# Depthwise taps of the first quarter ahead of the FFT rows, and full-height products in the inverse transform

## The chip, the core and the metric

The kernel runs on one core of a Trainium2 chip. Its engines are TensorE (PE, matrix products into PSUM), VectorE (DVE), ScalarE (ACT), GpSimd (POOL) and the queues that issue transfers (SP above all). Each works through its own list of instructions in order and waits on semaphores for the others. The metric is device time in microseconds (us) for one execution; less is better.

## What is computed

The reference is an H3 block with a long convolution, followed by a dense layer, both with a LayerNorm ahead and a residual:

```
k_shift = sum over t<4 of k delayed by t, times shift_k[:, t]       # depthwise taps
kv      = k_shift * v
y       = irfft(rfft(pad(kv)) * rfft(pad(ssm_k)))[:S] + kv * ssm_D  # FFT length 4096
h       = x + layernorm(x) * y
out     = h + relu(layernorm(h) @ w1) @ w2
```

The sequence has 2048 tokens of 512 channels, the dense layer is 1376 wide, inputs and output are bf16.

## The kernel before

The Fourier transforms are done as matrix products in two stages, 64 x 64. The cosine and sine tables are made on the chip: DVE computes angles as integers (`cs_turns`, `cc_turns`, `_turns`: an addition and a bit-wise AND each), and ACT takes sines of them (`table`, called through `cc_part` for the later pieces). POOL makes negated copies of the sine table (`negated`).

There is no automatic schedule: every engine runs its instructions in the order in which the program names them, so the order of the source is the order on each engine.

The stretch at the start, up to about 40 us:

- SP's queue issues the load of ssm_k (`sk`, 2 MB, L96), then transposing loads of k and v in quarters of 512 tokens, k0, v0, k1, v1 and so on (L113 to L118), then ssm_D (`draw`, L121). The tap weights (`wsh`, 4 KB) go through ACT's queue (L98).
- PE runs 22 warm-up matmuls on zeros (L110).
- POOL builds an identity, then for each of four channel groups the four diagonal matrices of tap weights (`wdiag`, L238), by which PE applies the taps.
- When ssm_k is there, `to_rows` (L277) turns it over: PE transposes words of two bf16 values (`pst`, L281) in eight groups, and DVE or ACT copies each group to the rows tile `kfl` (L284, L290; the letters D and A in L342 say who). PSUM holds three double banks (`ps0` to `ps2`, handed out in a ring by `place`) and two single ones (`pk0`, `pk1`).
- Then come eight rounds (L377). Round gb does the taps of two channel groups of quarter gb // 2 (`taps`: eight matmuls into `pk0` and `pk1`, and two DVE products with v from PSUM into `kvp2`, the place of kv in ssm_k's tile), and `stage1` of the FFT of ssm_k for eight columns: 64 small matmuls into two double banks, each copied to the table `a1` by ACT or DVE (`copy`, L259, L261). In rounds 0 to 5 ACT also takes one of six sines (`cc_part`).
- Then kv is turned to rows in the same way (L403 and L404), and stage 2 of ssm_k's transform follows, mixed with stage 1 of kv's (L410 to L421). Its DVE part adds ssm_D (`dtab`, which POOL prepares at L399) to the real part.

The product of the spectra and the inverse of stage 2 follow (L439 to L501). The inverse of stage 1 (`inv1`, L599) uses the tables `dre` and `dim`, of which the lower 64 rows hold a block for one half of the columns, the upper 64 rows for the other half, and the rest is zero. It multiplies the two halves of the rows separately: for each m and each of the two tables, two products with 64 rows and 128 columns, at two positions of PE's array. Sixteen steps b of four m each end in a copy to `ax`. `inv2_first` (L667) and the dense layer (`mlp1`, `mlp2`) follow and fill the rest, from about 110 us on.

Of the kernel before, what the change touches and what calls it, by code (L numbers as in the profile page):

```python
# [9 lines left out]
ALU = mybir.AluOpType  # L10
# [3 lines left out]
I32 = mybir.dt.int32  # L14
# [42 lines left out]
def kernel(  # L57
# [35 lines left out]


    sk = early.tile([P, DC, S], BF16, name="sk")
    nc.sync.dma_start(out=sk[:], in_=A_ssm_k.rearrange("(c p) t -> p c t", p=P))  # L96
    wsh = consts.tile([P, DC, KS], BF16, name="wsh")
    nc.scalar.dma_start(out=wsh[:], in_=A_shift_k.rearrange("(r p) j -> p r j", p=P))  # L98
    dtab = consts.tile([P, 64, DC], BF16, name="dtab")
    draw = consts.tile([P, DC, 64], BF16, name="draw")  # L100
    vT = [vp.tile([P, DC, 512], BF16, name=f"vT{c}") for c in range(4)]
# [1 line left out]
    kT = [(kvp if c < 2 else early).tile([P, DC, CH + 16], BF16, name=f"kT{c}") for c in range(4)]  # L103
    wdiag = kvp.tile([P, DC, KS, P], BF16, name="wdiag")

    idle = vT[3][:, 0, :]
    nc.vector.memset(idle, 0.0)
    warm = psum_t.tile([P, 512], F32, tag="pk0", name="warm")
    for _ in range(22):
        nc.tensor.matmul(out=warm[:], lhsT=idle[:, 0:P], rhs=idle, start=True, stop=True)  # L110

    nc.vector.memset(kT[0][:, :, 0:16], 0.0)
    for c in range(4):  # L113
        if c == 0:
            nc.sync.dma_start_transpose(out=kT[c][:, :, 16:CH + 16], in_=k_d[0:CH, :])  # L115
        else:
            nc.sync.dma_start_transpose(out=kT[c][:], in_=k_d[CH * c - 16:CH * c + CH, :])  # L117
        nc.sync.dma_start_transpose(out=vT[c][:], in_=v_d[CH * c:CH * c + CH, :])  # L118
    for dp in range(2):
        src = bass.AP(tensor=A_ssm_D.tensor, offset=A_ssm_D.offset + 64 * dp, ap=[[0, 64], [P, DC], [1, 64]])  # L120
        nc.sync.dma_start(out=draw[64 * dp:64 * dp + 64, :, :], in_=src)  # L121
# [28 lines left out]
    for s in range(0, P, 64):  # L150
# [5 lines left out]
    nc.gpsimd.memset(ident[:], 0.0)  # L156
    nc.gpsimd.affine_select(out=ident[:], in_=ident[:], compare_op=ALU.not_equal, fill=1.0,
                            base=0, pattern=[[-1, P]], channel_multiplier=1)
    ident32 = early.tile([P, P], F32, name="ident32")
    nc.gpsimd.tensor_copy(out=ident32[:], in_=ident[:])  # L160

    n1c = early.tile([P, 1], F32, name="n1c")
    n2c = early.tile([P, 1], F32, name="n2c")
# [14 lines left out]
    def at_k1(tab, k1):  # L178
        a, t = [p for p in tab if p[0] <= k1][-1]
        return t[:, k1 - a, :]  # L180

    tsn = early.tile([P, 32, 64], I32, name="w_ts")
    tcs = early.tile([P, 32, 64], I32, name="w_tc")
    ta = early.tile([P, 96], F32, name="w_ta")
# [18 lines left out]
    for dp in range(2):  # L203
        table(cs[0], tsn, dp)

    t1 = early.tile([P, 64], I32, name="f1_t")
    _turns(nc, t1[:, 0:32], r1[:], n1c[:], 128, True)
    _turns(nc, t1[:, 32:64], r1[:], n1c[:], 128, False)
    f1f = early.tile([P, 64], F32, name="f1_f")
    f1p = f1f[:].rearrange("p (k s) -> p s k", s=2)  # L210
    _sin(f1p[:, 0], t1[:, 0:32], 128)
    _sin(f1p[:, 1], t1[:, 32:64], 128, neg=True)
    t3 = early.tile([P, 2, 64], I32, name="dm_t")
    _turns(nc, t3[:, 0, :], r2[:, 32:96], n2s[:], 64, True)
    _turns(nc, t3[:, 1, :], r2[:, 32:96], n2s[:], 64, False)
    dsc = early.tile([P, 2, 64], F32, name="dm_f")
    cs_turns(*cs[1])
    cc_parts = [(cs[1], tsn, dp) for dp in range(2)] + [(p, tcs, dp) for p in cc for dp in range(2)]

    def cc_turns(a):  # L220
        part = tcs[:, a:a + 16, :]
        nc.vector.tensor_single_scalar(out=part, in_=tsn[:, a:a + 16, :], scalar=2048.0, op=ALU.add)
# [11 lines left out]
    for f in (f2hi, f2lo):  # L234
        nc.gpsimd.memset(f[:], 0.0)

    for rg in range(DC):
        nc.gpsimd.tensor_tensor(out=wdiag[:, rg, :, :], in0=ident[:].unsqueeze(1).to_broadcast([P, KS, P]),  # L238
                                in1=wsh[:, rg, :].unsqueeze(2).to_broadcast([P, KS, P]), op=ALU.mult)
        if rg == 1:  # L240
            nc.gpsimd.tensor_copy(out=f1hi[:, 0:64], in_=f1f[:])
            nc.gpsimd.tensor_tensor(out=f1f[:], in0=f1f[:], in1=f1hi[:, 0:64], op=ALU.subtract)
            nc.gpsimd.tensor_copy(out=f1lo[:, 0:64], in_=f1f[:])
# [27 lines left out]
    def bank2(name):  # L271
        return place([P, 2, 512], F32, name)
# [4 lines left out]
    def to_rows(word, q, fl, eng):  # L277
        shape = [P, 4, P]
        pst = tap_bank(q % 5 - 3, shape, F32, "pst") if word is sk_word and q % 5 > 2 else place(shape, F32, "pst")
        for i in range(4):  # L280
            nc.tensor.transpose(out=pst[:, i, :], in_=word(4 * q + i), identity=ident32[:])  # L281
        if eng == "D":
            fl32 = fl[:].rearrange("p g d n -> p (g d n)").bitcast(I32).rearrange("p (g d m) -> p g d m", g=64, d=2)
            nc.vector.tensor_single_scalar(out=fl32[:, :, :, 4 * q:4 * q + 4],  # L284
                                           in_=pst[:].bitcast(I32).rearrange("p m (d g) -> p g d m", d=2),
                                           scalar=0, op=ALU.bitwise_or)
        else:
            src = pst[:].rearrange("p m x -> p (m x)").bitcast(BF16).rearrange("p (m d g e) -> p d g m e", m=4, d=2, e=2)
            for d in range(2):
                nc.scalar.copy(out=fl[:, :, d, 8 * q:8 * q + 8].rearrange("p g (m e) -> p g m e", e=2), in_=src[:, d])  # L290
# [40 lines left out]
                             skip_group_check=True)  # L331


    kfl = early.tile([P, 64, 2, 64], BF16, name="kfl")
    sk32 = sk[:].rearrange("p c t -> p (c t)").bitcast(F32).rearrange("p (x m) -> p x m", m=32)
    kv32 = sk[:].rearrange("p c t -> p (c t)").bitcast(F32).rearrange("p (m x) -> p m x", m=32)

# [24 lines left out]


    kvp2 = sk[:].rearrange("p c t -> p (c t)").rearrange("p (m c a e) -> p m c a e", m=32, c=DC, e=2)
    def taps(c, h):
        pss = [tap_bank(i, [P, 512], F32, "pkv") for i in range(2)]
        for i in range(2):
            for j in range(KS):
                nc.tensor.matmul(out=pss[i][:], lhsT=wdiag[:, 2 * h + i, j, :],  # L369
                                 rhs=kT[c][:, 2 * h + i, 16 - j:CH + 16 - j], start=(j == 0), stop=(j == KS - 1))  # L370
        for i in range(2):
            nc.vector.tensor_tensor(out=kvp2[:, :, 2 * h + i, 8 * c:8 * c + 8, :].rearrange("p m a e -> p a m e"),  # L372
                                    in0=pss[i][:].rearrange("p (a m e) -> p a m e", a=8, e=2),
                                    in1=vT[c][:, 2 * h + i, :].rearrange("p (a m e) -> p a m e", a=8, e=2),
                                    op=ALU.mult)
# [222 lines left out]

    def inv1(b):  # L599
        if b < 15:  # L600
            ps = bank2("psi1")
            banks = (ps[:, 0], ps[:, 1])
        else:
            banks = (psum1.tile([P, 512], F32, tag="pm0", name="psi1a")[:], bank2("psi1b")[:, 0, :])
        for i in range(4):
            m = 4 * b + i
            for c, tab in ((0, dre), (1, dim)):
                for dp in range(2):
                    nc.tensor.matmul(out=banks[dp][:, 128 * i:128 * i + 128],  # L609
                                     lhsT=kf[halves[dp], c, 4 * m:4 * m + 4, :].rearrange("p r k -> p (r k)"),  # L610
                                     rhs=tab[halves[dp], dp].rearrange("p a b -> p (a b)"), start=(c == 0), stop=(c == 1),
                                     tile_position=(64 * dp, 0), skip_group_check=True)
# [231 lines left out]
```

## Time and profile before

| what | value |
|---|---|
| median of 3 runs | 203.83 us (203.73 to 203.92) |
| time of the profiled execution | 203.83 us |
| its span | 201.7 us |
| PE busy | 192.0 us (95%) |
| DVE busy | 145.3 us (72%) |
| ACT busy | 128.5 us (64%) |
| POOL busy | 86.5 us (43%) |

The span is the time between the first and the last instruction that the profile shows. A line of a timeline gives the start in us, the busy us, the engine, the line of the program, the operation, the tile written and the tile read, the shape, and how many instructions are merged; in brackets stands how long the engine was idle before it, and who released it. In the chain of work the columns are start, length and what ran. Names ending in q are an engine's issuing queue. An instruction that waits for a lock or a port after it started counts as busy, so its length may hold a wait.

### The profile page before, as it was taken

The numbers are of one execution on the slowest core, as the hardware profiler recorded it, in microseconds if no ns is written. First come the engines' busy times: TensorE is split into PE (matmuls) and PEld (weight loads), VectorE is DVE, ScalarE is ACT, GpSimd is POOL, SyncE is SP. The second block draws the span as 40 slices with busy tenths as digits, with TensorE's granted clock in tenths as the row PEclk, the third lists the DMA queues.
The fourth block names the chain that finished last, engine by engine and source line by source line (L and its number), as shares of the span: only waits on it lengthen the run. The fifth ranks groups of instructions, "written<-read, shape, count | busy, mean of one in ns | idle before, by whom it ended". The sixth has DMA issues, their size and how long they took to land.

```text
span 201.7 us, 5574 instructions
## 1 busy us (share of the span) xinstructions
PE 192.0 (95%) x2337; PEld 135.5 (67%) x2337; DVE 145.3 (72%) x238; ACT 128.5 (64%) x199; POOL 86.5 (43%) x121
## 2 busy tenths in 40 slices
PE   7799999999988999999999999999999999999991
PEld 2465555999977998987988877545664556544451
DVE  7998777887887998898994798968477127661131
ACT  2668899678785888885979865925570683036300
POOL 7599994000016999994959293301120002002000
PEclk9999999999999999999999999999999999999998
DMA  6999991000000007719981989744381702140011
GB/s 164 349 221 181 165 180 27 3 5 3 6 3 2 0 23 196 272 28 209 275 190 28 113 77 199 141 99 106 82 156 57 104 0 52 35 96 28 0 52 52
DMA packets 48492, 20.06 MB, mean 99 GB/s; under 512 B 43380, under 2 KB 46932, under 8 KB 48468
## 3 DMA queue, kind: packets, MB, share of 16 engines
q1 hardware_dynamic: 47940, 19.71, 48.1%
q8 instruction: 18, 0.29, 0.6%
q10 hardware_dynamic: 528, 0.00, 0.1%
q14 instruction: 6, 0.05, 0.1%
HBM read 7.08 MB, written 2.10 MB: 46 GB/s over the span
## 4 chain that ended last, share of the span: by engine, by line
PE 69%; SPq 10%; DVE 8%; DMA 5%; ACT 3%; issue 1%; POOL 1%; ACTq 0%
PE ps1m L716 19%; PE ps2m L746 19%; PE psy L462 6%; PE ps2k L328 4%; DMA kT<-in_A_k_dram 4%; SPq L115 4%; PE ps2k L330 4%; PE u L328 4%; PE u L330 3%; SPq L118 3%; SPq L117 3%; PE pz L689 3%; PE ps L310 2%; PE pst L281 2%; PE pkv L369 2%; DVE st L547 2%
## 5 line engine op out<-in xcount | busy, mean ns | idle before, releaser
L731 ACT ACTIVATE h1T<-ps1m 128x512 bf16<-128x512 f32 (+1 forms) x44 | 25.7, 597 | 35.8 <-PE ps1m L716 35.7
L716 PE MATMUL ps1m<-xT,w 128*128 128x512 bf16 (+2 forms) x192 | 43.7, 365 | 0.4 <-DVE xT L662 0.4
L746 PE MATMUL ps2m<-w,h1T 128*128 128x512 bf16 (+3 forms) x187 | 40.8, 368 | 0.0
L689 PE MATMUL pz<-bd,ax 128*128 128x128 f32 x96 | 35.7, 410 | 0.0
L452 POOL TENSOR_TENSOR t<-usb,kf 128x320 fp32r<-128x320 f32 x32 | 28.2, 930 | 2.2 <-ACT usb L448 1.7
L452 DVE TENSOR_TENSOR t<-u,kf 128x704 fp32r<-128x704 f32 x32 | 26.7, 884 | 3.3 <-ACT usb L448 3.2
L750 DVE SCALAR_TENSOR_TENSOR o<-ps2m,rstd,xh 128x512 bf16<-128x512 f32 (+1 forms) x17 | 12.1, 717 | 22.4 <-PE ps2m L746 11.5
L553 POOL TENSOR_SCALAR rstd<-mv 128x4 f32<-128x4 f32 x8 | 2.5, 317 | 57.1 <-DVE mv L551 57.1
L746 PEld LDWEIGHTS <-h1T 128*128 128x128 bf16 (+1 forms) x187 | 16.2, 98 | 16.0
L259 ACT CAST a<-ps 128x1024 fp32r<-128x1024 f32 (+1 forms) x22 | 22.4, 1053 | 2.8 <-PE ps L310 2.8
L716 PEld LDWEIGHTS <-w 128*128 128x128 bf16 (+1 forms) x192 | 15.9, 100 | 12.1 <-DVE xT L662 0.5
L689 PEld LDWEIGHTS pz<-bd,ax 128*128 128x128 f32 x96 | 18.6, 193 | 7.6
L547 DVE BATCH_NORM_STATS2 st<-xh 128x6 f32<-128x512 bf16 x32 | 19.9, 677 | 0.4 <-DMA xh<-xT 0.4
L660 DVE TENSOR_TENSOR qT<-pz,qT 128x1024 bf16<-128x1024 f32 x8 | 9.8, 1220 | 13.6 <-PE pz L689 10.8
L259 ACT CAST kf<-psy 128x512 fp32r<-128x512 f32 x30 | 17.5, 642 | 1.9 <-PE psy L462 0.2
L537 ACT ACTIVATE bd<-ecw,nbias 32x512 fp32r<-32x512 int32 x24 | 17.3, 719 | 0.6
L462 PE MATMUL psy<-t,ipos 128*128 128x512 f32 x48 | 16.0, 393 | 0.0
L369 PE MATMUL pkv<-kT,wdiag 128*128 128x512 bf16 x64 | 15.2, 380 | 0.6 <-POOL f_lo L247 0.4
L261 DVE CAST a<-ps 128x1024 fp32r<-128x1024 f32 (+1 forms) x12 | 13.6, 1136 | 2.7 <-PE ps L310 2.5
L259 ACT CAST ax<-psi 128x1024 fp32r<-128x1024 f32 x13 | 12.3, 1038 | 3.7 <-PE psi L609 3.5
L372 DVE TENSOR_TENSOR sk<-pkv,vT 128x512 bf16<-128x512 f32 x16 | 10.7, 689 | 4.5 <-PE pkv L369 4.1
L609 PE MATMUL psi<-dre,kf 64*128 64x128 f32 x120 | 13.8, 274 | 0.1
(132 smaller groups left out, 401.6 us busy)
## 6 DMA issues: line engine op xcount, KB each, us to landing
sk<-in_A_ssm_k_dram SPq DMA_DIRECT2D x1, 2048.0 KB
xh<-in_A_q_dram SPq DMA_DIRECT2D x16, 128.0 KB
out_dram<-o SPq DMA_DIRECT2D x15, 128.0 KB
w<-in_B_w_dram SPq DMA_DIRECT2D x1, 1376.0 KB
w<-in_B_w_dram SPq DMA_DIRECT2D x1, 1280.0 KB
xh<-xT SPq DMA_TRANSPOSE x8
out_dram<-o SPq DMA_DIRECT2D x2, 64.0 KB
w<-in_B_w_dram SPq DMA_DIRECT2D x1, 96.0 KB
```

Source lines behind the costliest of these rows:

```text
L259: nc.scalar.copy(out=o, in_=i)
L328: nc.tensor.matmul(out=ps[:, kk, :], lhsT=at_k1(w_re, k1), rhs=a_in(2 * k1), start=True, stop=False, skip_group_check=True)
L330: nc.tensor.matmul(out=ps[:, kk, :], lhsT=at_k1(w_im, k1), rhs=a_in(2 * k1 + 1), start=False, stop=True, skip_group_check=True)
L369: nc.tensor.matmul(out=pss[i][:], lhsT=wdiag[:, 2 * h + i, j, :], rhs=kT[c][:, 2 * h + i, 16 - j:CH + 16 - j], start=(j == 0), stop=(j == ...
L452: eng.tensor_tensor(out=t[:, :, j, :], in0=in0.unsqueeze(1).to_broadcast([P, 2, n, 2]), in1=kfr[:, :, j, ks], op=ALU.mult)
L462: nc.tensor.matmul(out=psy[:], lhsT=m_[:], rhs=t_.rearrange("p j k -> p (j k)"), start=first, stop=not first)
L537: nc.scalar.activation(out=bd[h][rows, :, :, rg, :], in_=ecw[q % 2][rows, :, 256 * h:256 * h + 256].rearrange("p b (j n) -> p b j n", n=32 ...
L547: nc.vector.bn_stats(out=st[:, i, :], in_=src[:, i, :])
L689: nc.tensor.matmul(out=pz[:, il, :, a, :], lhsT=ax[:, 64 * rho + n2, :, :].rearrange("p d g -> p (d g)"), rhs=bd[h][:, rho, 4 * il + a, :, ...
L716: nc.tensor.matmul(out=ps1[fc][:fsz, 128 * ii.start:128 * ii.stop].rearrange("p (i t) -> p i t", t=P), lhsT=w1[:, c, fc * P:fc * P + fsz], ...
L731: nc.scalar.activation(out=h1T[:fsz, fc, :], in_=ps1[fc][:fsz, :], func=ACT.Relu)
L746: nc.tensor.matmul(out=ps2[:, 0:w], lhsT=h1T[:ksz, fc, i * P:(i + 1) * P], rhs=w2[:ksz, fc, ds], start=(fc == 0), stop=(fc == NFC - 1))
```

## The change

- The load of the tap weights moves to SP's queue and stands first there; k's first quarter comes next, then ssm_k, then k and v of quarters 1 to 3, and v's first quarter last.
- The diagonals are built on POOL ahead of the second identity. PE runs 10 warm-up matmuls, then all tap products of quarter 0 into `pk0`, `pk1` and the double bank `ps2`, then 8 warm-up matmuls. DVE copies these sums to SBUF (`ks0`, bf16). The warm-up's zeros stand in the first rows of `kfl` instead of `vT3`.
- The angles of the small table f1 are computed ahead of the others; three of the six sines (both of the second `cs` piece, the first of `cc`) and `cc_turns(16)` go ahead of ssm_k's rows. The last of the three A groups of ssm_k's rows becomes a D group. `dsc` uses the bytes of `t3`.
- The rounds do the taps of quarters 1 to 3 in rounds 0 to 5, have none in rounds 6 and 7, and in round 7 the products of quarter 0 with v, two on DVE and two on POOL. Sines are left in rounds 0 to 2. `negated(22, 32)` stands ahead of the rounds.
- The inverse of stage 1 uses all 128 rows at once: two products of 128 rows and 256 columns for each m, zeros included, and copies that follow the new places of the results.

```diff
     sk = early.tile([P, DC, S], BF16, name="sk")
-    nc.sync.dma_start(out=sk[:], in_=A_ssm_k.rearrange("(c p) t -> p c t", p=P))
     wsh = consts.tile([P, DC, KS], BF16, name="wsh")
-    nc.scalar.dma_start(out=wsh[:], in_=A_shift_k.rearrange("(r p) j -> p r j", p=P))
+    nc.sync.dma_start(out=wsh[:], in_=A_shift_k.rearrange("(r p) j -> p r j", p=P))
...
-    idle = vT[3][:, 0, :]
+    kfl = early.tile([P, 64, 2, 64], BF16, name="kfl")
+    idle = kfl[:, 0:4].rearrange("p g d n -> p (g d n)")
     nc.vector.memset(idle, 0.0)
-    warm = psum_t.tile([P, 512], F32, tag="pk0", name="warm")
-    for _ in range(22):
-        nc.tensor.matmul(out=warm[:], lhsT=idle[:, 0:P], rhs=idle, start=True, stop=True)
+    def warm_up(n):
+        warm = psum.tile([P, 512], F32, tag="ps0", name="warm")
+        for _ in range(n):
+            nc.tensor.matmul(out=warm[:], lhsT=idle[:, 0:P], rhs=idle, start=True, stop=True)
+
+    warm_up(10)
...
+    load_k(0)
+    nc.sync.dma_start(out=sk[:], in_=A_ssm_k.rearrange("(c p) t -> p c t", p=P))
+    for c in (1, 2, 3):
+        load_k(c)
+        load_v(c)
+    load_v(0)
...
+    for rg in range(DC):
+        nc.gpsimd.tensor_tensor(out=wdiag[:, rg, :, :], in0=ident[:].unsqueeze(1).to_broadcast([P, KS, P]),
+                                in1=wsh[:, rg, :].unsqueeze(2).to_broadcast([P, KS, P]), op=ALU.mult)
     ident32 = early.tile([P, P], F32, name="ident32")
     nc.gpsimd.tensor_copy(out=ident32[:], in_=ident[:])
+
+    def tap_products(ps, c, rg):
+        for j in range(KS):
+            nc.tensor.matmul(out=ps, lhsT=wdiag[:, rg, j, :], rhs=kT[c][:, rg, 16 - j:CH + 16 - j], start=(j == 0),
+                             stop=(j == KS - 1))
+
+    ks0 = kvp.tile([P, DC, 512], BF16, name="ks0")
+    tap0 = [psum_t.tile([P, 512], F32, tag=f"pk{i}", name="tap0") for i in range(2)]
+    tap0b = psum.tile([P, 2, 512], F32, tag="ps2", name="tap0b")
+    tap0 = [t[:] for t in tap0] + [tap0b[:, i, :] for i in range(2)]
+    for rg in range(DC):
+        tap_products(tap0[rg], 0, rg)
+    warm_up(8)
...
-    dsc = early.tile([P, 2, 64], F32, name="dm_f")
+    dsc = t3[:].bitcast(F32)
...
+    for rg in range(2):
+        nc.vector.tensor_copy(out=ks0[:, rg, :], in_=tap0[rg])
+    cc_part()
+    cc_part()
     cc_turns(0)
+    for rg in range(2, 4):
+        nc.vector.tensor_copy(out=ks0[:, rg, :], in_=tap0[rg])
+    cc_part()
+    cc_turns(16)
...
-        to_rows(sk_word, q, kfl, "DADDADAD"[q])
-    cc_turns(16)
-    _sin(dsc[:], t3[:], 64)
+        to_rows(sk_word, q, kfl, "DADDADDD"[q])
+    _sin(dsc, t3[:], 64)
...
+    def by_v(eng, c, rg, ks):
+        eng.tensor_tensor(out=kvp2[:, :, rg, 8 * c:8 * c + 8, :].rearrange("p m a e -> p a m e"),
+                          in0=ks.rearrange("p (a m e) -> p a m e", a=8, e=2),
+                          in1=vT[c][:, rg, :].rearrange("p (a m e) -> p a m e", a=8, e=2), op=ALU.mult)
...
+    negated(22, 32)
     for gb in range(8):
-        taps(gb // 2, gb % 2)
+        if gb < 6:
+            taps(1 + gb // 2, gb % 2)
+        if gb == 7:
+            for rg in range(DC):
+                by_v((nc.vector, nc.gpsimd)[rg % 2], 0, rg, ks0[:, rg, :])
         stage1(kfl, a1k_of, gb, ("AA", "AD")[gb % 2], pairs=(gb == 2))
-        if gb < 6:
+        if gb < 3:
             cc_part()
-        if gb == 1:
-            negated(22, 32)
...
-            for c, tab in ((0, dre), (1, dim)):
-                for dp in range(2):
-                    nc.tensor.matmul(out=banks[dp][:, 128 * i:128 * i + 128],
-                                     lhsT=kf[halves[dp], c, 4 * m:4 * m + 4, :].rearrange("p r k -> p (r k)"),
-                                     rhs=tab[halves[dp], dp].rearrange("p a b -> p (a b)"), start=(c == 0), stop=(c == 1),
-                                     tile_position=(64 * dp, 0), skip_group_check=True)
+            for c, d in ((0, dre), (1, dim)):
+                nc.tensor.matmul(out=banks[i // 2][:, i % 2, :], lhsT=kf[:, c, 4 * m:4 * m + 4, :].rearrange("p r k -> p (r k)"),
+                                 rhs=d[:].rearrange("p d a b -> p (d a b)"), start=(c == 0), stop=(c == 1))
         if b < 15:
             copy("D" if b in (5, 10) else "A", ax[:, :, :, 4 * b:4 * b + 4],
-                 ps[:].rearrange("p d (i x) -> p x d i", i=4))
+                 ps.rearrange("p b i (d x) -> p x d (b i)", d=2))
         else:
-            for dp, eng in enumerate("AD"):
-                copy(eng, ax[:, :, dp, 60:64], banks[dp].rearrange("p (i x) -> p x i", i=4))
+            for h, eng in enumerate("AD"):
+                copy(eng, ax[:, :, :, 60 + 2 * h:62 + 2 * h], banks[h].rearrange("p i (d x) -> p x d i", d=2))
```

More of the change, by code (lines that the diff above doesn't have):

```diff
@@ L104, with load_k @@
     wdiag = kvp.tile([P, DC, KS, P], BF16, name="wdiag")
-    idle = vT[3][:, 0, :]
+    kfl = early.tile([P, 64, 2, 64], BF16, name="kfl")
+    idle = kfl[:, 0:4].rearrange("p g d n -> p (g d n)")
     nc.vector.memset(idle, 0.0)
-    warm = psum_t.tile([P, 512], F32, tag="pk0", name="warm")
-    for _ in range(22):
-        nc.tensor.matmul(out=warm[:], lhsT=idle[:, 0:P], rhs=idle, start=True, stop=True)
+    def warm_up(n):
[3 more added lines that the diff above has]
+    warm_up(10)
     nc.vector.memset(kT[0][:, :, 0:16], 0.0)
-    for c in range(4):
+    def load_k(c):
         if c == 0:
@@ L117, with load_v @@
             nc.sync.dma_start_transpose(out=kT[c][:], in_=k_d[CH * c - 16:CH * c + CH, :])
+    def load_v(c):
         nc.sync.dma_start_transpose(out=vT[c][:], in_=v_d[CH * c:CH * c + CH, :])
+    load_k(0)
[4 more added lines that the diff above has]
+    load_v(0)
     for dp in range(2):
@@ L180, in at_k1 @@
         return t[:, k1 - a, :]
+    t1 = early.tile([P, 64], I32, name="f1_t")
+    _turns(nc, t1[:, 0:32], r1[:], n1c[:], 128, True)
+    _turns(nc, t1[:, 32:64], r1[:], n1c[:], 128, False)
+    f1f = early.tile([P, 64], F32, name="f1_f")
+    f1p = f1f[:].rearrange("p (k s) -> p s k", s=2)
+    _sin(f1p[:, 0], t1[:, 0:32], 128)
+    _sin(f1p[:, 1], t1[:, 32:64], 128, neg=True)
     tsn = early.tile([P, 32, 64], I32, name="w_ts")
@@ L204 @@
         table(cs[0], tsn, dp)
[L206 to L212, printed above, removed]
     t3 = early.tile([P, 2, 64], I32, name="dm_t")
@@ L235 @@
         nc.gpsimd.memset(f[:], 0.0)
[L237 to L243, printed above, removed]
+    nc.gpsimd.tensor_copy(out=f1hi[:, 0:64], in_=f1f[:])
+    nc.gpsimd.tensor_tensor(out=f1f[:], in0=f1f[:], in1=f1hi[:, 0:64], op=ALU.subtract)
+    nc.gpsimd.tensor_copy(out=f1lo[:, 0:64], in_=f1f[:])
     for f, g in ((f1hi, f2hi), (f1lo, f2lo)):
@@ L331, in stage2 @@
                              skip_group_check=True)
-    kfl = early.tile([P, 64, 2, 64], BF16, name="kfl")
     sk32 = sk[:].rearrange("p c t -> p (c t)").bitcast(F32).rearrange("p (x m) -> p x m", m=32)
@@ L367, in taps @@
         for i in range(2):
-            for j in range(KS):
-                nc.tensor.matmul(out=pss[i][:], lhsT=wdiag[:, 2 * h + i, j, :],
-                                 rhs=kT[c][:, 2 * h + i, 16 - j:CH + 16 - j], start=(j == 0), stop=(j == KS - 1))
+            tap_products(pss[i][:], c, 2 * h + i)
         for i in range(2):
[L372 to L375, printed above, removed]
+            by_v(nc.vector, c, 2 * h + i, pss[i][:])
+    negated(22, 32)
     for gb in range(8):
-        taps(gb // 2, gb % 2)
+        if gb < 6:
[3 more added lines that the diff above has]
+                by_v((nc.vector, nc.gpsimd)[rg % 2], 0, rg, ks0[:, rg, :])
         stage1(kfl, a1k_of, gb, ("AA", "AD")[gb % 2], pairs=(gb == 2))
-        if gb < 6:
+        if gb < 3:
             cc_part()
-        if gb == 1:
-            negated(22, 32)
     pl.pop("psT")
@@ L600, in inv1 @@
         if b < 15:
-            ps = bank2("psi1")
+            ps = bank2("psi1").rearrange("p b (i x) -> p b i x", i=2)
             banks = (ps[:, 0], ps[:, 1])
         else:
-            banks = (psum1.tile([P, 512], F32, tag="pm0", name="psi1a")[:], bank2("psi1b")[:, 0, :])
+            banks = [t.rearrange("p (i x) -> p i x", i=2)
+                     for t in (psum1.tile([P, 512], F32, tag="pm0", name="psi1a"), bank2("psi1b")[:, 0, :])]
         for i in range(4):
             m = 4 * b + i
-            for c, tab in ((0, dre), (1, dim)):
-                for dp in range(2):
-                    nc.tensor.matmul(out=banks[dp][:, 128 * i:128 * i + 128],
-                                     lhsT=kf[halves[dp], c, 4 * m:4 * m + 4, :].rearrange("p r k -> p (r k)"),
-                                     rhs=tab[halves[dp], dp].rearrange("p a b -> p (a b)"), start=(c == 0), stop=(c == 1),
-                                     tile_position=(64 * dp, 0), skip_group_check=True)
+            for c, d in ((0, dre), (1, dim)):
+                nc.tensor.matmul(out=banks[i // 2][:, i % 2, :], lhsT=kf[:, c, 4 * m:4 * m + 4, :].rearrange("p r k -> p (r k)"),
+                                 rhs=d[:].rearrange("p d a b -> p (d a b)"), start=(c == 0), stop=(c == 1))
         if b < 15:
             copy("D" if b in (5, 10) else "A", ax[:, :, :, 4 * b:4 * b + 4],
-                 ps[:].rearrange("p d (i x) -> p x d i", i=4))
+                 ps.rearrange("p b i (d x) -> p x d (b i)", d=2))
         else:
-            for dp, eng in enumerate("AD"):
-                copy(eng, ax[:, :, dp, 60:64], banks[dp].rearrange("p (i x) -> p x i", i=4))
+            for h, eng in enumerate("AD"):
+                copy(eng, ax[:, :, :, 60 + 2 * h:62 + 2 * h], banks[h].rearrange("p i (d x) -> p x d i", d=2))
     lift(0)
```

## The prediction

> **What bounds the kernel now.** I read the page first, then the chain of work that ended last in order of time, then the timelines of the engines for the first 40 us and for the inverse stage, because the diff touches these two stretches and nothing else. The chain in its early part:
>
> ```profile
> 21.56 7.64 DMA kT<-in_A_k_dram
> 29.25 1.91 PE pkv L369 x8
> 31.15 0.61 PE ps L310 x64
> 31.77 1.90 PE pkv L369 x8
> 33.70 0.70 DVE sk L372
> 34.54 3.88 PE pst L281 x32
> ```
>
> It blames k's last quarter, which lands just before the taps at 29.25. But PE had ended its work just before, so three things run equally late there: loads, PE, ACT. Relieving one alone brings little. What opens the loop is DVE:
>
> ```profile
> 7.81 1.21 DVE L189 TENSOR_SCALAR w_ts<-w_ts 128x640 int32<-128x640 int32 x1
> 8.94 1.53 DVE L222 TENSOR_SCALAR w_tc<-w_ts 128x1024 int32<-128x1024 int32 x1
> 10.50 0.69 DVE L189 TENSOR_SCALAR w_tc<-w_tc 128x1024 int32<-128x1024 int32 x1
> 11.11 3.08 DVE L284 TENSOR_SCALAR kfl<-pst 128x512 int32<-128x512 int32 x5
> 14.11 0.69 DVE L222 TENSOR_SCALAR w_tc<-w_ts 128x1024 int32<-128x1024 int32 x1
> ```
>
> DVE has no gap from 0.85 to 16.7. ssm_k's words have been ready for it since PE began transposing them at 9.17, yet it copies the first to rows at 11.11, when its table arithmetic ends, and the fifth ends at 14.19. The products of ssm_k need all rows. In PE's timeline, by shape:
>
> ```profile
> 9.17 2.48 PE L281 MATMUL pst<-ident,sk 128*128 128x128 f32 x20 [1.06 <-DMA sk<-in_A_ssm_k_dram]
> 13.30 1.89 PE L369 MATMUL pkv<-kT,wdiag 128*128 128x512 bf16 x8
> 15.12 0.21 PE L310 MATMUL ps<-f_hi,kfl 32*128 32x64 bf16 x4
> ```
>
> So the first product is at 15.12 and kv's transposes at 34.54: 19.42 us for eight rounds. ACT is nearly full in them:
>
> ```profile
> 15.87 2.05 ACT L259 CAST a<-ps 128x1024 fp32r<-128x1024 f32 x2 [1.45 <-PE ps L310]
> 25.58 1.25 ACT L193 ACTIVATE c2c<-w_tc,hbi,hsc 128x1024 fp32r<-128x1024 int32 x1
> 31.88 2.01 ACT L259 CAST a<-ps 128x1024 fp32r<-128x1024 f32 x2
> ```
>
> The profiled execution took 203.83 us, the median of the runs itself; its span is 201.7, with 2.13 around it. All sums go against it.
>
> **Part 1, until the first product.** Every table instruction ahead of the rows stays. DVE gets four new copies of tap sums from PSUM (128x512; the kf copies of that shape on L261 take 0.69), 2.7 us, and cc_turns(16), two instructions of 0.69 that so far came after the rows, 1.4 us. Both stand ahead of the first row copy: 11.11 + 4.1 = 15.2. Six row copies of 0.62 follow instead of five (ACT gives up one word group of 1.07): the last ends at 18.9. PE's first taps of the loop need the tap bank that the row copies free at about 17 and take 1.85, to 19.1. First product at 19.2 instead of 15.12: **+4.1**.
>
> What else moves here hides behind that DVE queue:
> - *Loads.* On SP's queue the tap weights' issue (0.46 on ACT's now) and k's first transpose (2.1 to 2.5 where a transpose is not stretched by a 2 MB load) go ahead of ssm_k: it lands at about 9.2 + 2.8 = 12, at most 13 if the small load isn't overlapped. Cover until 15.2: 2 to 3 us. Without cover it would cost what it is late. Bytes are the same, so the last load (now v's first quarter) lands when v's last did, 31.0, or 1 us later. Its products (DVE 2 x 0.69 beside POOL 2 x 1.04) end by 34.1. kv is wanted at 36.8, so there are 2.7 us of cover; k's and v's other quarters come one transpose earlier relative to their use.
> - *PE.* 18 warm-up matmuls instead of 22; chunk 0's 16 tap matmuls (3.7 us) run from about 6.3, when k's quarter and the first diagonal are there, to 10; eight warm ones to 12. Free, as PE waits for DVE until 17. The tap sums sit in three of the banks that the rows' transposes use, so the third to fifth word groups wait in PE's queue for DVE's four copies; DVE wants these groups only after the copies.
> - *ACT.* Three sines (0.91, 0.91, 1.25) go ahead of the rows. They follow DVE's turns and end near 14; its first row copy of 1.07 is then earlier than DVE's.
> - *POOL.* The diagonals go ahead of ident32, the long negation (3.45) ahead of the loop, two products of v0 ahead of the dre/dim scaling. That tail (4.77 without waits) ends near 39; its reader, the kf addition, stood at 39.62 and moves to about 41.9: 3 us of cover.
> - The zeros in ssm_k's rows, and dsc in t3's bytes: no new instruction; the rows' first writer stands behind the warm-up matmuls anyway. Nothing.
>
> *The unknown here* is DVE against POOL. The 640-element wrap above takes 1.21 where 1024 elements take 0.69, and the 1024-element addition 1.53 instead of 0.69, both while POOL builds two diagonals; 0.8 + 0.8 = 1.6 us are lost that way. Now four diagonals (1.04 each) fall into DVE's busy time. None lost: -1.6; all four in full: 4.2 - 1.6 = +2.6. I take no difference, the two rows being of the same instructions.
>
> The Trainium skill ("SBUF — State Buffer", Who interferes with whom) states that the two engines lock a shared port for whole instructions. These rows agree; by that rule a negation of 2.80 us (POOL L250) could stop one of the cc_turns(16) instructions, and the sum would be 2.8 higher.
>
> **Part 2, from first product to kv's transposes.** PE loses two pairs of taps, 3.7 us; if PE set the pace, 15.7 would remain. ACT sets it: first copy 0.75 after the first product, 12 copies of 1.02, three sines of 1.25: 0.75 + 12.2 + 3.8 = 16.8. Products use two of three PSUM places, so round n+1 needs round n's first copy. The last two rounds have no taps to fill that time: product 0.6 and hand-over 0.25 before ACT has work, twice, +1.7. The transposes need round 6's copies but not round 7's, -1.0. That is 17.5, **-1.9**. Bounds: 15.7 (PE alone) and 19.42 (nothing saved). I stay near ACT's sum, as ACT has hardly a gap in this stretch now. kv's transposes at 34.54 + 4.1 - 1.9 = 36.7; everything behind (stage 2, products, MLP) follows PE or kv and shifts by that **+2.2**.
>
> **Part 3, inverse stage 1.** From the waits and PE's timeline:
>
> ```profile
> 93.20 0.19 PEld L609 LDWEIGHTS psi<-dim,kf 64*128 64x128 f32 x2
> 93.26 0.28 PE L609 MATMUL psi<-dim,kf 64*128 64x128 f32 x2
> 93.37 0.27 PE L609 MATMUL psi<-dre,kf 64*128 64x128 f32 x2
> ```
>
> A pair of 64-row products comes every 0.111 us; 128 pairs make 14.2 us. The new form is 128 products of 128 rows by 256 columns. Nearest rows: ps2k L328/L330 at 41 to 43 us, same shape and contiguous operand, every 0.114; u L328 with a strided operand 0.12. So +0.4 to +1.15; PE now waits 0.35 us for copies inside the stage (before 100.41 and 105.98), which may absorb some. I take **+0.3** (contiguous operand), bounds -0.3 and +1.15. Copies stay 15 of the same size and two halves. If the copies bind instead, it is nothing.
>
> The Trainium skill ("TensorEngine Tiling (Array Packing)", Key Properties) says that row tiles work in parallel, so a pair should last as one product of 128 columns. The rows say otherwise: a pair costs as much as 256 full-height columns. By the rule the change would lose half of 128 x 0.114, 7.3 us; by the rows 0.3.
>
> **Sum:** 4.1 - 1.9 + 0.3 = +2.5 on 203.83: 206.3 us.
>
> **Rivals.**
> - *More lock waits.* A diagonal or a negation stops the turns more often: rows up to 2.6 later than forecast: 208.9. For it: the 1.53 row. Against it: POOL's small copies stand between the diagonals and the negations.
> - *Faster: PE's saving is kept whole.* If lock waits vanish (first product at 17.6, +2.5) and ACT keeps up so that the rounds fall to PE's 15.7 (-3.7): -1.2 + 0.3, 202.9. It decides from first products before 17 to 18.5 together with rounds of 16 us or less. For it: the sines leave the loop. Against it: ACT's sum of 16.8.
> - *Loads bind.* v's first quarter lands after 34.6 (36.7 less POOL's two products) instead of near 31.5; at 36 kv would be ready at 38.1, 1.4 late: 207.7. For it: it is last in the queue. Against it: the same bytes end at 31 now.
> - *No net change:* both bounds half way, 203.8.
>
> **Chances:** forecast (within about 1.2 us of 206.3) 0.61; more lock waits 0.18; loads bind 0.04; no net change 0.05; faster 0.12. The likeliest case's own range is 205.1 to 207.5. The 8-in-10 range is 203.9 to 208.7: it leaves out the faster case, and of the lock waits' case the upper half. About 0.2% (0.4 us) is what a measurement of this kernel can tell from no change: faster 0.13, same 0.04, slower 0.83.
>
> **What would show it.** Right: DVE's row copies of ssm_k start at 15 to 16 while ssm_k's transposes began near 12; the first product near 19, kv's transposes near 36.7; psi matmuls every 0.114 to 0.12. Wrong: row copies before 13.5, or ssm_k landing after 15 (then loads, not DVE, open the loop), or eight rounds in less than 16.5 us.

## The result and the profile after

The changed kernel takes 208.68 us (median of 4 runs, 208.09 to 214.08) against 203.88 us (203.73 to 204.03) for the kernel before on the same chip: ratio 1.0226 [1.0203, 1.0249], 4.6 us slower. The 214.08 us is one execution in a slower state (mean TensorE clock 0.968, against 0.992 to 1.000 in the others), and such executions are left out of every ratio. The profiled execution took 208.62 us, its span is 206.8 us, 5.1 more than before; outside the span 0.3 us came back (1.8 instead of 2.1). Where the span grew, by the starts of the same work in the two traces:

| start of | before | after | later by | step's share |
|---|---|---|---|---|
| first row copy of ssm_k | 11.11 | 16.77 | 5.66 | +5.66 |
| first product of stage 1 | 15.12 | 21.59 | 6.47 | +0.81 |
| kv's transposes | 34.54 | 39.13 | 4.59 | -1.88 |
| column means before the inverse's stage 1 | 91.83 | 96.44 | 4.61 | 0.0 |
| first `pz` behind the inverse's stage 1 | 109.78 | 114.60 | 4.82 | +0.2 |
| first product of the dense layer (`ps1m`) | 114.05 | 119.22 | 5.17 | +0.35 |

The chain of work that ended last, in order of time (start, length, what ran), in its early part:

```profile
14.98 1.16 DVE w_tc L250
...
17.51 2.42 PE pst L313 x12
19.93 1.73 PE pkv L179 x8
...
30.17 1.84 PE pkv L179 x8
32.01 0.61 PE ps L342 x64
32.62 1.84 PE pkv L179 x8
34.46 0.69 PE ps L342 x64
35.15 1.11 ACT a L291
36.30 0.74 PE ps L342 x62
37.05 1.05 ACT a L291
...
39.13 3.88 PE pst L313 x32
```

DVE, then PE, then the copies of the last rounds: no load stands in it. The rounds with taps follow each other at PE's pace, 1.84 + 0.61 = 2.45 us each (a bit more for the round of pairs). The end is slow, where no taps are left: from round 5's products at 34.39 to kv's transposes 4.7 us pass, in which PE works for 2.1 (0.69 + 0.74 + 0.66) and waits for ACT's copies otherwise.

DVE's timeline of the changed kernel until the rows (start, busy, what; `w_ta`, `w_ts` and `w_tc` are table arithmetic, `ks` the new copies of tap sums):

```profile
3.08 1.02 DVE L220 TENSOR_SCALAR w_ta<-w_r,n2c 128x32 f32<-128x32 int32 x1
4.02 1.09 DVE L221 TENSOR_SCALAR w_ta<-w_r,n2c 128x64 f32<-128x64 int32 x1
5.14 2.40 DVE L233 TENSOR_TENSOR w_ts<-w_ta 128x1408 int32<-128x1408 f32 x1
7.57 1.61 DVE L224 TENSOR_SCALAR w_ts<-w_ts 128x1408 int32<-128x1408 int32 x1
...
11.18 1.28 DVE L257 CAST ks<-tap 128x512 bf16<-128x512 f32 x2
...
12.38 0.68 DVE L250 TENSOR_SCALAR w_tc<-w_ts 128x1024 int32<-128x1024 int32 x1
...
13.70 1.28 DVE L262 CAST ks<-tap0b 128x512 bf16<-128x512 f32 x2
14.90 1.23 DVE L250 TENSOR_SCALAR w_tc<-w_ts 128x1024 int32<-128x1024 int32 x1
16.16 0.69 DVE L224 TENSOR_SCALAR w_tc<-w_tc 128x1024 int32<-128x1024 int32 x1
16.77 2.59 DVE L316 TENSOR_SCALAR kfl<-pst 128x512 int32<-128x512 int32 x4
```

An instruction on 32 elements cannot need 1.02 us when one on 1024 takes 0.69: the first four lines hold waits. POOL's timeline shows what runs at that time, and the late use of v's first quarter:

```profile
3.00 5.44 POOL L172 TENSOR_TENSOR wdiag<-ident,wsh 128x512 bf16<-128x512 bf16 x4
...
14.53 8.05 POOL L282 TENSOR_SCALAR c2n<-c2s 128x1024 fp32r<-128x1024 f32 x3
...
30.95 2.28 POOL L396 TENSOR_TENSOR sk<-ks,vT 128x512 bf16<-128x512 bf16 x2 [4.44 <-DMA draw<-in_A_ssm_D_dram]
```

The four diagonals end at 8.44; behind them DVE's instructions have their usual length, but for one: the first of `cc_turns(16)` at 14.90 takes 1.23 us, where its twin at 12.38 takes 0.68, and POOL's long negation has begun at 14.53. So that line holds a wait of 0.55 us too. PE's timeline, the lines that answer those of before:

```profile
11.85 1.13 PE L313 MATMUL pst<-ident,sk 128*128 128x128 f32 x8 [0.59 <-POOL f_hi L279]
15.04 2.12 PE L313 MATMUL pst<-ident,sk 128*128 128x128 f32 x12 [2.06 <-DVE ks L262]
17.51 2.42 PE L313 MATMUL pst<-ident,sk 128*128 128x128 f32 x12 [0.35 <-DVE kfl L316]
...
21.59 0.21 PE L342 MATMUL ps<-f_hi,kfl 32*128 32x64 bf16 x4
...
39.13 3.88 PE L313 MATMUL pst<-ident,sk 128*128 128x128 f32 x32 [0.32 <-issue]
```

ssm_k is there at 11.85, so PE is ready long before DVE. The 12 transposes at 17.51 take 2.42 us; in the kernel before 12 of them take 1.61:

```profile
11.85 1.61 PE L281 MATMUL pst<-ident,sk 128*128 128x128 f32 x12 [0.20 <-DVE kfl L284]
```

A table by windows says why (window, length, busy us and instructions of PE, PEld, DVE, ACT, POOL, then the granted PE clock, the DMA share and GB/s):

```profile
10.00:15.00 5.00, 2.39 (x14) 1.36 (x12) 4.93 (x10) 5.00 (x6) 4.49 (x11) 1.00 1.16 275
16.00:19.30 3.30, 2.94 (x15) 2.55 (x15) 3.25 (x6) 1.39 (x4) 3.30 (x2) 0.50 1.03 212
```

PE was busy for 2.39 of the 5 us before 15; from 15.95 to 19.36, which is 3.41 us, its clock was granted by half. The kernel before has 1.00 there, with PE busy for 4.80 of the 5 us before 15.

ACT is no longer full in the rounds. Its timeline:

```profile
22.45 2.07 ACT L291 CAST a<-ps 128x1024 fp32r<-128x1024 f32 x2 [3.89 <-PE ps L342]
...
32.68 2.04 ACT L291 CAST a<-ps 128x1024 fp32r<-128x1024 f32 x2 [0.81 <-PE ps L342]
```

And the inverse's stage 1, one product of 128 rows and 256 columns every 0.12 us where a pair of half-height products came every 0.11:

```profile
96.44 1.34 PE L530 MATMUL pm<-w,ones 128*128 128x344 bf16 x8
97.74 0.28 PE L642 MATMUL psi<-dim,kf 128*128 128x256 f32 x1
97.86 0.28 PE L642 MATMUL psi<-dre,kf 128*128 128x256 f32 x1
...
114.60 3.86 PE L708 MATMUL pz<-ecore,ax 32*128 32x256 f32 x128 [0.32 <-DVE ax L293]
```

### The profile page after: what moved, and what is told of

It is laid out like the page before. It is cut to its first block, busy times and chain, and to the rows that moved or that the text cites. A ratio compares the mean times of both kernels' runs of the same rounds, so it can differ in the third digit from the quotient of the medians.

```text
span 206.8 us, 5309 instructions
## 1 busy us (share of the span) xinstructions
PE 193.2 (93%) x2205; PEld 136.9 (66%) x2205; DVE 148.8 (72%) x241; ACT 127.9 (62%) x197; POOL 89.6 (43%) x123
## 4 chain that ended last, share of the span: by engine, by line
PE 84%; DVE 9%; ACT 3%; issue 1%; POOL 0%; POOLq 0%; ACTq 0%
PE ps1m L747 19%; PE ps2m L777 19%; PE psy L495 7%; PE psi L642 7%; PE pkv L179 5%; PE ps L342 5%; PE ps2k L360 4%; PE ps2k L362 4%; PE u L360 3%; PE u L362 3%; PE pst L313 3%; PE pz L720 3%; ACT a L291 2%; DVE w_ts L233 2%; DVE w_ts L224 1%
## 5 line engine op out<-in xcount | busy, mean ns | idle before, releaser
L642 PE MATMUL psi<-dre,kf 128*128 128x256 f32 x60 | 14.6, 286 | 0.0
L642 PE MATMUL psi<-dim,kf 128*128 128x256 f32 x60 | 14.2, 280 | 0.0
L313 PE MATMUL pst<-ident,sk 128*128 128x128 f32 x64 | 9.5, 309 | 3.3 <-DVE ks L262 2.1
```

Of the source, the lines that this page charges most:

```text
L642: nc.tensor.matmul(out=banks[i // 2][:, i % 2, :], lhsT=kf[:, c, 4 * m:4 * m + 4, :].rearrange("p r k -> p (r k)"), rhs=d[:].rearrange("p ...
```

## The experiments

Every kernel below computes the whole reference. Ratios are against the kernel before on the same chip, with 95% intervals; the changed kernel itself stands at 1.0226. The chips of these runs were a little slower (medians of the kernel before 204.84, 204.66 and 205.03 us), so ratios are compared, not times.

**1 and 2: which part carries the loss.** First the kernel before with only the new inverse stage 1, then the changed kernel with the old one:

```diff
-                for dp in range(2):
-                    nc.tensor.matmul(out=banks[dp][:, 128 * i:128 * i + 128], ..., tile_position=(64 * dp, 0), ...)
+                nc.tensor.matmul(out=banks[i // 2][:, i % 2, :], lhsT=kf[:, c, 4 * m:4 * m + 4, :]..., rhs=d[:]..., ...)
```

> The kernel before with only the full-height inverse stage 1. Theory (the early stretch carries the loss): the stage from the first psi product to the first pz product grows by 0.3 to 0.6 us, so 204.2 to 204.5 us. Rival (the inverse stage carries a good part of the 4.8 us, because zeros are multiplied too): 1.2 us or more, 205.1 us or above. If the copies to ax set the pace: no change, 203.9.

> The changed kernel with the old inverse stage 1, so the early part alone. Theory: 0.3 to 0.6 us less than the changed kernel, 208.1 us, kv's transposes still at 39.1 us. Rival (inverse): 207.5 us or less.

Measured: the new inverse alone 205.21 us, 1.0012 [0.9993, 1.0030]; the old inverse in the changed kernel 208.27 us, 1.0187 [1.0144, 1.0229]. PE's timeline of the first of the two, from the column means to `pz`:

```profile
92.31 1.34 PE L497 MATMUL pm<-w,ones 128*128 128x344 bf16 x8
...
110.46 3.86 PE L675 MATMUL pz<-ecore,ax 32*128 32x256 f32 x128 [0.31 <-DVE ax L261]
```

That stretch takes 18.15 us here, 18.16 in the changed kernel, 17.95 before, and 17.97 with the old form put back. So the inverse costs 0.2 us in its stage and at most 0.6 us in time; the loss lies in the first 40 us. The second kernel also shows PE's clock at 1.00 at 16 us, with nothing altered there:

```profile
15.05 1.61 PE L313 MATMUL pst<-ident,sk 128*128 128x128 f32 x12 [1.68 <-DVE ks L262]
17.53 1.62 PE L313 MATMUL pst<-ident,sk 128*128 128x128 f32 x12 [0.86 <-DVE kfl L316]
```

The 12 transposes take 1.62 us instead of 2.42, the first product starts at 20.8 instead of 21.59, kv's transposes at 38.37 instead of 39.13. That prices the half clock at this place: 0.8 us.

**3: keep PE warm.** Twenty warm-up matmuls instead of eight behind quarter 0's taps.

```diff
-    warm_up(8)
+    warm_up(20)
```

> The changed kernel with 20 instead of 8 warm-up matmuls behind the taps of the first quarter, so that PE is idle for less than 1.5 us before the rows' transposes go on. Theory (about 1.0 us of the loss is PE at half clock from 16 to 19.4 us, as its idle time before that lowered the granted clock): granted clock 1.00 throughout, the last twelve transposes of ssm_k take about 1.5 instead of 2.42 us, first product at 20.7 instead of 21.7, 207.7 us. Rival (DVE's queue alone sets the first product, the clock is incidental): first product stays at 21.5 or later, 208.6 us.

Measured: 210.25 us, 1.0261 [1.0223, 1.0298], not faster. The early part went as expected: clock 1.00 at 16 us, first product at 20.80. The gain was lost further on, in PE's timeline:

```profile
25.36 1.90 PE L179 MATMUL pkv<-kT,wdiag 128*128 128x512 bf16 x7 [1.43 <-DVE a L293]
...
39.66 5.05 PE L313 MATMUL pst<-ident,sk 128*128 128x128 f32 x32 [0.24 <-issue]
```

Before the taps of round 2 PE issues nothing for 1.43 us; the weight loads of the same moment are put down to "issue", that is to nothing the profile shows. (The copy that the row names as releaser is hardly the cause: in the changed kernel, with the same order behind the warm-up, the same taps start at 24.65, ahead of that copy at 24.82.) Then the clock is halved from 39.06 to 42.47 and kv's transposes take 5.05 us instead of 3.88. Why PE stood still stays open. The half clock alone does not explain the missing gain: two of the four executions had a mean clock of 1.000 and took 209.49 and 209.69 us, 1.023 times the kernel before, no better than the changed kernel.

**4: take POOL's diagonals out of DVE's way.** ACT builds them, 16 small instructions; the taps of quarter 0 and the warm-up follow them in the program.

```diff
-    for rg in range(DC):
-        nc.gpsimd.tensor_tensor(out=wdiag[:, rg, :, :], in0=ident[:]..., in1=wsh[:, rg, :]..., op=ALU.mult)
+    wsh32 = consts.tile([P, DC, KS], F32, name="wsh32")
+    nc.gpsimd.tensor_copy(out=wsh32[:], in_=wsh[:])
...
     _sin(f1p[:, 1], t1[:, 32:64], 128, neg=True)
+    for rg in range(DC):
+        for j in range(KS):
+            nc.scalar.activation(out=wdiag[:, rg, j, :], in_=ident[:], func=ACT.Copy, scale=wsh32[:, rg, j:j + 1])
```

> The changed kernel with the sixteen diagonals built by ACT, which is idle from 3.5 to 9.2 us, instead of POOL. Theory (four POOL products stop DVE's table instructions, which lost about 3 us in all from 3 to 9.2 us): the two small w_ta instructions fall from 2.1 to 0.5 us, the 1408-element addition from 2.4 to 1.65, the first row copy of ssm_k from 16.8 to about 14.5, total 206.5 us. Rival (DVE was slow for another reason, for instance the transfers into SBUF at that time): these instructions keep their lengths, total 208.6 us.

Measured: 206.31 us, 1.0078 [1.0049, 1.0108]: 1.5%, some 3 us, of the loss is gone. DVE's timeline of this kernel, the four instructions that held waits and the first row copies:

```profile
3.08 0.28 DVE L222 TENSOR_SCALAR w_ta<-w_r,n2c 128x32 f32<-128x32 int32 x1
3.27 0.28 DVE L223 TENSOR_SCALAR w_ta<-w_r,n2c 128x64 f32<-128x64 int32 x1
3.59 1.63 DVE L235 TENSOR_TENSOR w_ts<-w_ta 128x1408 int32<-128x1408 f32 x1
5.25 0.89 DVE L226 TENSOR_SCALAR w_ts<-w_ts 128x1408 int32<-128x1408 int32 x1
...
13.53 3.67 DVE L318 TENSOR_SCALAR kfl<-pst 128x512 int32<-128x512 int32 x6
```

0.28, 0.28, 1.63 and 0.89 us for what took 1.02, 1.09, 2.40 and 1.61 beside POOL: 3.04 us of waiting, and the first row copy moves from 16.77 to 13.53. The clock is 1.00 as well in this execution, in which the tap sums are copied 2.9 us sooner and PE does not stand between the transposes; the other five have mean clocks of 0.980 to 0.992, and four of them took about as long (206.03 to 206.46 us, against 206.22). With the rows this early the loads do begin to bind: DVE waits 0.80 and 1.35 us for v, and the rounds take 18.46 us (17.80 to 36.26). The chain of this kernel follows the queue of loads until a quarter of v lands at 28.9:

```profile
22.87 6.03 DMA vT<-in_A_v_dram
...
28.99 0.70 DVE sk L398
```

So with DVE's waits gone, the new order of loads is the next limit.

The Trainium skill ("SBUF — State Buffer", Who interferes with whom) says that where DVE works in a mode with two ports, whichever of DVE and POOL issues first holds the shared port pair for its whole instruction and the other stands still. The first two rows agree, though no run shows the mode they worked in: beside diagonals of some 1.4 us (5.44 for four), each of the two small instructions lasted about 1 us instead of 0.28.

**5: the last turns behind the rows.** `cc_turns(16)` goes back behind ssm_k's row copies.

```diff
     cc_part()
-    cc_turns(16)
...
         to_rows(sk_word, q, kfl, "DADDADDD"[q])
+    cc_turns(16)
```

> The changed kernel with cc_turns(16) behind ssm_k's row copies, where it stood before. Theory (every instruction ahead of the row copies in DVE's list delays the first product by its own length and its waits for POOL): first row copy at 14.9 instead of 16.8, first product about 1.5 to 1.9 us earlier, kv's transposes near 37.4 instead of 39.1, total 1.5 us less, 0.7 of a per cent. Rival (rows wait for something else, for instance PE's banks or ACT's two row copies): less than 0.5 us.

Measured: 211.3 us (median of 212.69, 211.63, 210.98 and 208.37), 1.0245 [1.0190, 1.0301] by the last two, no gain. The one at a mean clock of 1.000 is 208.37 us, 1.018, about 0.5 us better than the changed kernel at full clock (208.09 us, 1.0206 on its chip), one execution against one. The profile is of the execution with 212.69 us, so it shows where that one lost its time. The first row copy is at 14.91, 1.9 us earlier, as expected. But in this execution the transposes fell into a half-clock stretch (15.13 to 18.55; 24 of them in 4.54 us), and the turns now run beside POOL's long negation (14.55 to 22.2). DVE's timeline:

```profile
20.54 0.89 DVE L250 TENSOR_SCALAR w_tc<-w_ts 128x1024 int32<-128x1024 int32 x1
21.47 1.78 DVE L224 TENSOR_SCALAR w_tc<-w_tc 128x1024 int32<-128x1024 int32 x1
```

2.67 us instead of 1.4, ahead of the products with v that free the tap banks. PE's timeline shows who pays (the same wait returns in experiment 7):

```profile
23.89 1.89 PE L179 MATMUL pkv<-kT,wdiag 128*128 128x512 bf16 x8 [1.95 <-DVE sk L396]
```

The half clock came again from 39.02 to 45.85, and kv's transposes, at 40.64, lasted 6.22 us.

**6: does ACT set the pace of the rounds?** The three sines that are left in rounds 0 to 2 go ahead of the rounds.

```diff
     _sin(dsc, t3[:], 64)
+    for _ in range(3):
+        cc_part()
...
-        if gb < 3:
-            cc_part()
```

> The changed kernel with its last three sines ahead of the rounds, where ACT is idle from 18.6 to 22.5 us. Theory (ACT sets the pace of the rounds, 12 copies and three sines): from first product to kv's transposes 16.0 to 16.5 instead of 17.5 us, total 1.0 to 1.5 us less. Rival (PE, banks or the empty last rounds set the pace): 17.3 us or more in the rounds, no change.

Measured: 208.99 us, 1.0213 [1.0176, 1.0250]. The first product starts at 21.62, and PE's timeline has kv's transposes at

```profile
39.09 3.88 PE L313 MATMUL pst<-ident,sk 128*128 128x128 f32 x32 [0.34 <-issue]
```

17.5 us as before the edit, with 3.8 us less for ACT to do in the rounds. ACT does not set the pace of the rounds with taps; its copies in the last rounds, which follow no sine, are untouched by this edit.

**7: both together.** The diagonals on ACT, `cc_turns(16)` behind the rows, and the old inverse (the diffs of 4, 5 and 2).

> The changed kernel with the diagonals on ACT, cc_turns(16) behind the row copies and the old inverse stage 1. Theory: each part adds its own gain until the loads bind: v's first quarter lands at about 32.4, its products end at 34.7, kv's transposes near 35.2, total about 0.3 us above to 0.5 us below the kernel before. Rival (the new order pays as soon as DVE's delay is gone): kv's transposes at 33.5, 1 us below the kernel before.

Measured: 209.44 us, 1.0227 [1.0197, 1.0256], worse than 4 alone. The first product came at 17.68, but the turns again met the negation (1.27 and 1.77 us), and PE's timeline shows the next taps:

```profile
20.60 3.55 PE L178 MATMUL pkv<-kT,wdiag 128*128 128x512 bf16 x8 [2.24 <-DVE sk L398]
```

PE stood for 2.24 us and went on at half clock (20.59 to 24.0): 3.55 us for eight taps that take 1.89. Even their start is 2.2 us behind that in experiment 4 (18.41), though the first product came at the same time there (17.80). kv's transposes came at 38.99. So the place of `cc_turns(16)` ahead of the rows, which costs 1.5 us there, is the cheaper of the two.

**8: shorten the two rounds without taps.** In rounds 5 to 7 each double bank is copied half by ACT, half by DVE.

```diff
-        stage1(kfl, a1k_of, gb, ("AA", "AD")[gb % 2], pairs=(gb == 2))
+        stage1(kfl, a1k_of, gb, ("AD", "AD") if gb > 4 else ("AA", "AD")[gb % 2], pairs=(gb == 2))
```

> The changed kernel with the copies of rounds 5, 6 and 7 split between ACT and DVE in halves. Theory, formed after the sines ahead of the rounds changed nothing (PE sets the pace of rounds 0 to 5, and the last rounds, which have no taps, run from copy to copy): from the product of round 5 to kv's transposes about 3.7 instead of 4.7 us, total 0.8 to 1.0 us less than the changed kernel. Rival (v's first quarter or its products set the end): no change.

Measured: 210.8 us, 1.0293 [1.0251, 1.0336], slower. DVE's timeline:

```profile
34.87 1.29 DVE L293 CAST a<-ps 128x512 fp32r<-128x512 f32 x2 [0.57 <-ACT a L291]
36.96 1.29 DVE L293 CAST a<-ps 128x512 fp32r<-128x512 f32 x2 [0.80 <-ACT a L291]
```

DVE's half waits for ACT's half of the same double bank (ACT's start at 34.25 and 36.34), so the two halves run one after the other, while in round 5 of the changed kernel ACT and DVE copy one whole double bank each side by side (from 35.13 and 35.18). The tail takes 5.8 us instead of 4.7, part of it at half clock (36.99 to 43.81); 0.45 us of the difference falls ahead of the last products, the first that PE runs at half clock (two steps of 2.11 and 2.09 us instead of 1.91 and 1.84). The products with v's first quarter were done before the end (POOL 33.0; DVE's 38.17 in the middle of the copies), so the tail follows the copies and not the loads.

The Trainium skill ("PSUM — Partial Sum Buffer", PSUM bank collisions raise a hardware error) says that the compiler's scheduler puts an order between two engines that use the same bank. These two rows agree with it, but no run here tells that order from one that the two halves of the destination would cause.

**9: an attempt at a faster version.** The diagonals on ACT, two of the four tap-sum copies on ACT, one sine moved back into the rounds, rounds 0 and 4 (instead of 6 and 7) without taps, the old inverse.

```diff
+    for rg in range(2):
+        nc.scalar.copy(out=ks0[:, rg, :], in_=tap0[rg])
...
-    for rg in range(2):
-        nc.vector.tensor_copy(out=ks0[:, rg, :], in_=tap0[rg])
...
-        if gb < 6:
-            taps(1 + gb // 2, gb % 2)
...
+        if gb not in (0, 4):
+            t = gb - 1 - (gb > 4)
+            taps(1 + t // 2, t % 2)
```

> Diagonals on ACT, two of the four tap sums copied by ACT, four sines in the rounds, rounds 0 and 4 without taps (the last round has some), v's first quarter multiplied ahead of round 7's taps, old inverse stage 1. Theory: first row copy near 12.8, first product near 16.6, PE busy without a gap from then on, kv's transposes at 34 to 35, total within 0.5 us of the kernel before on either side. Rival (PE's idle time brings the half clock again): over 1 us slower than before, granted clock below 0.995.

Measured: 206.98 us, 1.0082 [1.0049, 1.0115], no better than 4. First row copy 13.31, first product 17.55: here the rows wait for ssm_k itself, whose transposes start at 12.59 after 1.68 us of waiting for its load. kv's transposes came at 36.59, since a round without taps waits for copies wherever it stands (PE had almost nothing from 26 to 27.7 in round 4, ACT's copies coming behind a sine). No version here beats the kernel before.

## Why the prediction was right in its direction and short by 2.4 us

- **First row copy (predicted 15.2, measured 16.77).** The DVE sum held: the four tap-sum copies take 1.20 + 1.20 = 2.4 us in the chain (predicted 2.7), and `cc_turns(16)` without waits 1.3 (1.4), as its twin `cc_turns(0)` does (12.46 to 13.79). The term that was mis-sized is "I take no difference" for the waits on POOL. The run with the diagonals on ACT gives the count: beside the four diagonals DVE lost 3.04 us, where the prediction read 1.6 beside two of them in the kernel before, so four cost about twice what two cost. Another 0.55 us went beside the long negation: it did stop an instruction of `cc_turns(16)`, as the prediction had considered, but not for its whole 2.8 us. Together +2.0, inside the bounds of -1.6 to +2.6 but near the upper one; less 0.4 for the smaller copies and turns that is the 1.6 by which the row copy was late.
- **First row copy to first product (predicted 4.0, measured 4.8).** With PE at full clock it is 4.0 (16.79 to 20.8 in the run with the old inverse). The other 0.8 us is the half clock from 15.95 on, which the prediction did not have among its terms. The step that left it out is "Free, as PE waits for DVE until 17", which put PE's idle time at nothing. That the idle time brought the half clock is not shown: the run with the old inverse has the same work and nearly the same gap (1.68 us instead of 2.06) and kept its clock. First product +6.5 instead of +4.1: 2.0 of waits, 0.8 of clock, less 0.4 of smaller copies and turns.
- **Rounds (predicted 17.5, measured 17.54).** The size was right, the reason was not. "ACT sets it" is refuted for the rounds with taps: without ACT's three sines all rounds together took the same 17.5. PE sets the pace as long as there are taps (12.8 us, 21.59 to 34.39), and the tail without them takes 4.7 us, of which PE needs 2.1. The prediction's terms come to about 13.7 for the first six rounds (0.75, nine copies, three sines) and 3.8 for the tail (three copies, +1.7 and -1.0); the two errors of 0.9 cancelled, which was luck.
- **Loads (no cost predicted).** ssm_k is used from 11.85 (about 12 forecast), the taps of quarter 0 start at 5.70 (6.3), the products with v's first quarter end at 33.2 on POOL and 37.4 on DVE, ahead of kv's transposes at 39.13; the chain holds no load. But ssm_k comes some 3 us later than before (in these runs its transposes begin at 11.85 to 12.6 instead of 9.17), and this is hidden only behind DVE's queue: in the runs in which DVE was ready sooner, v cost DVE 0.80 and 1.35 us (diagonals on ACT), and the last attempt's rows waited for ssm_k.
- **Inverse stage 1 (predicted +0.3).** +0.2 in the stage, 1.0012 in time. The rows decided rightly against packing: a pair of half-height products of 128 columns had been as long as one full one of 256.
- **Not foreseen at all:** from `pz` to the first product of the dense layer 4.62 us instead of 4.27. It goes with the early part (4.62 with the old inverse too, 4.28 with the new inverse alone). In the kernels with the new early part DVE's first instruction there (`qT`) starts when ACT's fourth piece of `bd` ends (114.86 in experiment 4), before it started 0.40 us after the third; why is open.
- **Rivals.** What happened is the rival "More lock waits" by 2.0 of its 2.6 us, with the clock in place of the rest: 208.7 against its 208.9. The measured 208.68 lies outside the likeliest case's own range (205.1 to 207.5) and 0.02 us inside the wide one (203.9 to 208.7); that it is inside is luck, as executions of this kernel differ by more than that (208.09 to 208.73). The faster rival fell with the first product at 21.59, where it needed 17 to 18.5.

## What to carry to other kernels

A step that takes work off PE and puts copies on the engine that opens the critical path has to be counted on that engine first; here 3.7 us of taps left the rounds, 1.9 came back as time, and DVE paid 5.7 ahead of them. Before a POOL instruction is moved, look at which DVE instructions will stand beside it: the same four diagonals cost DVE 3 us beside table arithmetic and nothing when ACT made them. Idle time on PE may not be free: a stretch with PE half idle was followed by 3.41 us at half clock in three of five kernels with the same work there. Once the first queue is relieved, look at what stood behind it, here the loads. And rounds that no longer hold matmuls to cover a copy show the copy in full.

## What the runs showed of the hardware that was not expected

- **The half clock comes in pieces of 3.41 us (or two of them), and the order of work alone does not settle whether.** Five kernels have the same work on PE up to the transposes at 15.04; PE's idle time before them was 1.68, 1.78, 1.79, 1.83 and 2.06 us, and the clock was halved behind the second, fourth and fifth, not behind the first and third. With the wait for ssm_k just before (0.97, 0.88, 0.86, 0.82 and 0.59 us) all five come to 2.65 us of idle time. One kernel's own runs differ too: the changed kernel took 208.09 us at a mean clock of 1.000 and 208.62 at 0.992. One piece of 3.41 us at half clock in a span of 207 us makes a mean of 0.992 by these numbers, but what it costs depends on where it falls: 0.5 to 0.6 us here, nothing that can be seen with the diagonals on ACT (206.22 at 1.000; 206.03, 206.04, 206.41 and 206.46 at 0.992). The Trainium skill ("TensorE: Matmul & The Clock Gate", Part 1: The HAM clock gate) gives a window of about 3.4 us that runs on its own and is not aligned to the kernel; the length agrees with 3.41, and the phase, which would fit these differences, is not shown by any run here.
- **DVE instructions on 32 and 64 elements wait for POOL like large ones** (0.28 alone, 1.02 and 1.09 us beside the diagonals). Beside a negation of POOL the wait is irregular: the 0.69 us instruction took 0.87, 0.89, 1.23, 1.27, 1.77 or 1.78.
- **PE may stand for 1.43 us with nothing in the profile to release it**, when twelve more warm-up matmuls ahead shift the rest (experiment 3); open.
